# A gated mix of recurrent attention and a GEGLU feed-forward: buffers, order of a step, and the Wo group changed together

## The chip, the core and the metric

The kernel runs on one core of one Trainium2 chip. A core has five engines that run their own instruction streams and wait for each other through semaphores: TensorE (PE, matmuls into the eight PSUM banks), VectorE (DVE), ScalarE (ACT), GpSimd (POOL) and SyncE (SP, which here only issues DMAs). SP, ACT and POOL all issue DMAs, and each of them issues in the order of its own stream. The metric is the time of one execution on the device in microseconds.

## The reference: what is computed

Two branches work on the same x (2048 rows of 1024, bf16) and are mixed row by row:

```python
def _A_ref(x, mem0, Wq, Wk, Wv, Wo, seg_len):      # 32 heads of 128, seg_len 32, memory of 8 rows
    mem = mem0
    for s in range(n_seg):                          # 64 segments, one after the other
        h = concat([mem, x[s*32:(s+1)*32]])         # 40 rows
        q, k, v = h @ Wq, h @ Wk, h @ Wv            # each 1024 x (32 x 128)
        p = softmax(masked(q @ k.T * scale))        # rows see the memory and what is before them
        o = (p @ v) @ Wo
        mem = o[:8]                                 # the next segment's memory
        outs.append(o[8:])
def _B_ref(x, w_gate, w_up, w_down):                # 1024 -> 3584 -> 1024
    return gelu(x @ w_gate) * (x @ w_up) @ w_down
g = sigmoid((x * gate_w).sum(-1))
return g * a + (1 - g) * b
```

The attention branch is a recurrence: segment s+1 needs the first eight rows of segment s's output. Its weights (four matrices of 8 MB) don't fit in SBUF together.

## The kernel before, in words

**A planner, not hand-placed semaphores.** `op(eng, fn, rd, wr, lane)` records every operation with the byte ranges of SBUF, the PSUM banks and the DRAM pieces that it reads and writes. `_Prog.finish` (L118) derives the waits from that; `emit` (L135) writes each engine's stream in the order of recording. A DMA has a lane, that is, a semaphore. After its last operation SP waits for the last value of every lane (L153). What sets the order of the work is therefore the order of the calls, and what makes something wait is an overlap of bytes, banks or lanes.

**Four phases.** First the feed-forward branch, in four blocks of 512 rows (`for fb in range(NFB)`, L1060): 28 rounds j of gate and up matmuls into two pairs of banks, each followed by gelu on ACT and DVE into GT; then two passes `ps` over w_down in chunks of WD, the second pass backwards in the first three blocks so that the buffers left from the first are used at once. `mix` scales a finished bank by 1 - g and stores it to b_scr. Between rounds stand the preparations of x: `do_x` (PE transposes 128 rows; ACT and DVE copy them out in two forms; ACT issues the stores to xq_scr and xr_scr), `dot_x` (POOL multiplies by gate_w, DVE sums), `gate` (the sigmoid) and, in the last block, `begin(n)`, which loads the first attention weights into slots as FFN buffers come free.

Then step 0 of the recurrence with the projections of rows that need no memory ("fills", below), then 63 more steps, then the output phase: the remaining rows' Wo product (L1189), `blend` and the stores.

**Slots and pieces.** SBUF beyond the small tiles is 50 slots of 4096 bytes a partition. A piece is 512 KB of Wk, Wq, Wv or Wo: (m, u, i) is matrix m, half u of the heads, piece i of 8. Some pieces of the two halves share a slot (`PAIRS`, L317: two of k, two of q, five of v, five of o: 0, 1, 4, 5, 6). A shared slot is reloaded once a step, as soon as PE has done with it. `spent` (L440) counts the uses; neighbouring shared pieces are loaded by one DMA when the last of them is spent (`GROUPS`, L373, `load_group`, L422). SP issues all of these.

**A step.** `HEAD` and `BODY` (L324) give PE's order: k of the first half of the heads (r=0) pieces 0-3, q 0-1, the previous step's second Wo product pieces 4-7, q 2-3, v 0-3, k, q, v 4-7; then k, q (r=1), Wo (r=0), v (r=1), and the first four pieces of the second Wo product. In that second product the pieces come in the order 2, 3, 0, 1, 7, 4, 5, 6. `plan(s)` (L955) hangs everything else on this walk: `on(m, r, n, f)` runs f before piece n of (m, r). So `on("q", 0, 2, f)` puts f before q's third piece.

**Fills and stages.** Of each segment's 32 rows only the last 8 are not in the step's own projection; they are projected four segments at a time, in "fills" (L907). Each group of four steps needs six, listed in `FILL` (L945); steps 0 and 1 of four have two. The second of two is run and copied out by ACT at the start of the next step (`fill_evac`), into a stage of 1024 bytes a partition: stage 0 lies over hT0 and oRc, stage 1 over oRc and hT1. `fill_put` (L924) turns it on PE (L732), copies it back with DVE (L930) and stores it to qk_scr with a DMA on POOL (L932); it does nothing for v. Later in the same step, at ("q", 1, 1), ACT copies the step's own k, second half, into the same stage, and at ("o", 0, 0) PE turns that. `load_h` and `rest_o` use the bytes after that.

The last step moves five Wo pieces into slots of k and q (`late`), for the output phase.

Of the kernel before, what the change touches and what calls it, by code (L numbers as in the profile page):

```python
# [30 lines left out]
class _Prog:  # L31
# [73 lines left out]
    def finish(self):  # L105
        cnt = {e: 0 for e in self.ENGS}
        clocks = {e: {} for e in self.ENGS}
        for o in self.ops:
            if o.sem is None and o.need:
                cnt[o.eng] += 1  # L110
                o.sem, o.val, o.inc = self.sems[o.eng], cnt[o.eng], 1
        for o in self.ops:
            ck = clocks[o.eng]
            want = {}
            for d in o.deps:
                if ck.get(d.sem, 0) >= d.val:
                    continue
                if want.get(d.sem, (0, None))[0] < d.val:  # L118
                    want[d.sem] = (d.val, d)
            if want:  # L120
                items = sorted(want.items(), key=lambda kv: -kv[1][1].idx)
                ck = dict(ck)
                for s, (v, d) in items:
                    if ck.get(s, 0) >= v:
                        continue
                    o.waits.append((s, v))
                    for s2, v2 in d.clock.items():
                        if ck.get(s2, 0) < v2:
                            ck[s2] = v2
                    if ck.get(s, 0) < v:  # L130
                        ck[s] = v
                clocks[o.eng] = ck
            o.clock = ck

    def emit(self, block):  # L135
        self.finish()
        by = {e: [o for o in self.ops if o.eng == e] for e in self.ENGS}
        finals = [(ln[0], ln[1]) for ln in self.lanes.values()]
# [72 lines left out]
def bass_gated_mix__memory_aug_recurrent_mem_tr__geglu_ffn__prompt_kernel(  # L211
# [34 lines left out]
    with ExitStack() as es:  # L246
# [126 lines left out]
        GROUPS = {("k", 0): 2, ("q", 0): 2, ("v", 0): 3, ("v", 3): 2, ("o", 0): 1, ("o", 1): 1, ("o", 4): 3}  # L373
# [105 lines left out]
        WD = 4  # L479
# [6 lines left out]
        wd = [al(f"wd{i}", [128, WD, D]) for i in range(3)]  # L486
# [20 lines left out]
        xT = al("xT", [128, TB, 4, KC, SEG])  # L507
        assert cur[0] == edge(29)
# [3 lines left out]
        assert cur[0] == edge(43)  # L512
        osbF = [al(f"osbF{t}", [128, D], at=edge(28) + 2 * D * t) for t in range(2)]
        wdF = al("wdF", [128, NJ, D], at=edge(29))
        GT = al("GT", [128, NJ, FB])
        assert cur[0] == edge(50) and len(hosts) == 50
        for n in range(4):
            stage[f"X{n}"] = al(f"X{n}", [128, 512], at=edge(49) + 1024 * n)
        for n in range(3):
            stage[f"Y{n}"] = al(f"Y{n}", [128, 512], at=kT.off + 1024 * n)  # L520
        tp = [al(f"tp{t}", [128, FB], FP32, at=qkr.off + 4 * FB * t) for t in range(2)]
# [23 lines left out]
        def do_x(T):  # L545
            t = px[T % NPX]
            b = T % 2 + (4, 4, 0, 4)[T // TB]
# [4 lines left out]
            def f(e):  # L552
# [10 lines left out]
            op("dve", lambda e: e.tensor_copy(to, PBV[b].rearrange("p (k i c) -> p k i c", k=KC, i=4)[:, :, :, NR:SEG]),  # L563
               rd=[BK(b)], wr=[to_r])

            def put():
                op("act", lambda e: e.dma_start(xq_scr[T, :, :, :], xo[0].rearrange("p i k c -> p i (k c)")),
                   rd=[xo[1](0, 4)], wr=[("D", "xq", T)], lane=f"xw{x2}")
                if T > 0:
                    op("act", lambda e: e.dma_start(xr_scr[T], to.rearrange("p k i c -> p (k i c)")),  # L570
# [6 lines left out]
        def dot_x(T):  # L577
            t = px[T % NPX]
            op("pool", lambda e: e.tensor_tensor(out=gp[:, :], in0=t[:, :], in1=gwb[:, :], op=ALU.mult),
               rd=[t.r(), gwb.r()], wr=[gp.r()])  # L580
            op("dve", lambda e: e.tensor_reduce(dl[:, T:T + 1], gp[:, :], AX.X, ALU.add), rd=[gp.r()], wr=[dl.r(T, T + 1)])
# [35 lines left out]
        def load_wd(c):  # L617
            op("sp", lambda e: e.dma_start(wd[c % 3][:, :, :],
                                           B_w_down[c * WD * 128:(c + 1) * WD * 128, :].rearrange("(j p) f -> p j f", p=128)),
               wr=[wd[c % 3].r()], lane=f"wd{c % 3}")  # L620
# [11 lines left out]
        def gate(fb):  # L632
            c = slice(TB * fb, TB * fb + TB)
            r = lambda t: t.r(TB * fb, TB * fb + TB)
            op("act", lambda e: e.activation(gal[:, c], dl[:, c], ACTF.Tanh, scale=0.5), rd=[r(dl)], wr=[r(gal)])
            op("dve", lambda e: e.tensor_scalar(out=oml[:, c], in0=gal[:, c], scalar1=-0.5, scalar2=0.5, op0=ALU.mult, op1=ALU.add),
# [11 lines left out]
        jF = {1: (0, 1), 6: (1, 3), 13: (3, NWD)}  # L648

        def load_wdF(c):  # L650
            op("sp", lambda e: e.dma_start(wdF[:, c * WD:(c + 1) * WD, :],
                                           B_w_down[c * WD * 128:(c + 1) * WD * 128, :].rearrange("(j p) f -> p j f", p=128)),
               wr=[wdF.r(c * WD * D, (c + 1) * WD * D)], lane=f"wd{c % 3}")
# [9 lines left out]
        op("pe", tr_mem, rd=[pm.r(), mT.r(), ident.r()], wr=[BK(6)])  # L663
        op("dve", lambda e: e.tensor_copy(mS[:, 72:80], PBV[6][:, 64:64 + NB]), rd=[BK(6)], wr=[mS.r(72, 80)])
        op("dve", lambda e: e.tensor_copy(memT[:, :], PBV[6][:, 0:64]), rd=[BK(6)], wr=[memT.r()])

# [40 lines left out]
        def blend(T):  # L707
# [4 lines left out]
            op("act", lambda e: e.dma_start(of[128 * T:128 * T + 128, :], t[:, 0:D]), rd=[t.r(0, D)], wr=[("D", "out", T)], lane=f"ol{T % 4}")  # L712
# [242 lines left out]
        def plan(s):  # L955
# [11 lines left out]
            if s == 0:  # L967
                on("v", 0, 0, lambda: fill0("v", 0, B2, "X3"))
# [15 lines left out]
            if s == 0:  # L984
                on("k", 1, 0, lambda: load_v(0, slice(0, 1)))
            on("k", 1, 1 if s == 0 else 4, lambda: evac(bank_of["v", 0], vA, "act"))
            if s == 0:
                on(*('k', 1, 4), lambda: scores(ua, False))
                on("k", 1, 1, lambda: fill0("k", 1, A1, "X0"))
                on(*('q', 1, 2), lambda: attend(ua))  # L990
                on("k", 1, 4, lambda: fill_put("k", 1, 0, "X0"))
                on("q", 1, 0, lambda: fill0("q", 1, B1, "X1"))
                on("q", 1, 2, lambda: fill_put("q", 1, 0, "X1"))
                on("q", 1, 4, lambda: load_qk(0, 1))
                on("q", 1, 4, lambda: fill0("v", 1, B2, "X2"))
                on("q", 1, 4, lambda: load_r(1) if NG > 1 else None)
                on("o", 0, 4, lambda: load_v(0, slice(1, 2)))
# [34 lines left out]
            if last:  # L1032
                late = [lambda k=k, n=n: load_piece(moved[k], k, f"moved{n}") for n, k in enumerate(moved)]
                on("q", 0, 4, *late[:3])
                on("v", 0, 4, *late[3:])
# [16 lines left out]
            if two:  # L1052
                on("q", 0, 2, lambda: fill_put(*fl[1], ua, SS), **nx)
# [6 lines left out]
        for fb in range(NFB):  # L1060
            HB, DN = ((0, 1, 2, 3), (4, 5, 6, 7)) if fb % 2 == 0 else ((4, 5, 6, 7), (0, 1, 2, 3))
            for j in range(NJ):
# [24 lines left out]
                if todo and j % 3 == 2:  # L1087
                    mix(*todo.pop(0))
                if fb == 0 and j < TB:
                    puts.pop(0)()  # L1090
                    dot_x(j)
                    load_x(j + NPX)
                if fb == 0 and j == TB - 1:
                    load_w(3)
                    load_w(4)
                    for n in range(3):
                        load_wd(n)
                if fb == 0 and j == TB:
                    gate(0)
# [3 lines left out]
                if fb < NFB - 1 and j in (6, 11, 16, 21):  # L1103
                    do_x(T)
                    dot_x(T)
                    load_x(T + NPX)
                if fb < NFB - 1 and j == 25:
                    gate(fb + 1)
# [7 lines left out]
            if fb + 1 == NFB:  # L1116
                for n in (11, 12, *range(20, 28)):
                    begin(n)
            for ps in range(NPS):
# [4 lines left out]
                for c in range(NWD)[::-1 if back else 1]:  # L1124
                    w = wdF if end else wd[c % 3]
# [14 lines left out]
                    if not end:  # L1140
                        if back and c == 3:
                            load_xT(fb + 1)
                        nc_ = c - 3 if back else c + 3
                        if 0 <= nc_ < NWD:
                            load_wd(nc_)
                    elif ps == NPS - 1:
                        for f in {1: [lambda: fill0("k", 0, A0, "Y0")],
                                  2: [lambda: fill0("k", 0, A1, "Y1", 1, hR1), lambda: fill_put("k", 0, 0, "Y0")],
                                  3: [lambda: fill0("q", 0, XO, "Y2"), lambda: fill_put("k", 0, 1, "Y1")],
                                  4: [lambda: fill_put("q", 0, 0, "Y2")], 5: [lambda: load_qk(0, 0)]}.get(c, ()):  # L1150
                            f()
                        for n in (29 + 2 * c, 30 + 2 * c, 43 + c):
                            if n < 49:
                                begin(n)
# [3 lines left out]
        begin(28)  # L1158
# [22 lines left out]
        for b in range(NBK):  # L1181
            ob = orb[0]
            for hf in range(2):
# [10 lines left out]
                while mixed < NT and mixed < 2 * (2 * b + hf) + 4:  # L1194
# [6 lines left out]
                   rd=[ob.r(lo, hi)], wr=[("D", "out", T) for T in range(4 * b, 4 * b + 4)], lane=f"or{hf}")  # L1201
# [37 lines left out]
```

## Time and profile before

| | |
|---|---|
| median of three runs | 2202.14 us (2199.84 to 2203.8) |
| the profiled execution | 2196.2 us, its span 2194.4 us |
| feed-forward, 12 to 620 us | PE busy 595.9 of 608; DMA share 0.52 |
| end of it and step 0, 620 to 671 us | PE busy 36.6 of 51; granted clock 0.87 |
| steps 1 to 61, 671 to 2079 us | PE busy 1300.1 of 1408; DMA share 0.93, 347 GB/s |
| last two steps, 2079 to 2131 us | PE busy 40.4 of 52; granted clock 0.89 |
| output phase, 2131 to 2194.4 us | PE busy 55.6 of 63.4 |

The stretches were chosen by the first and last instruction of each phase. "PE busy" is the union of its matmuls; the DMA share is the mean busy share of the core's 16 DMA engines; the granted clock is the share of TensorE's full clock that the profile records. In the lines of waits, "A <- B: 24.5, 34, 1.6" says that A's engine sat idle for 24.5 us in all, 34 times, at most 1.6, until B was done. In the timeline a line has start, duration, engine, line of the code, what is written and read, how many instructions, and in brackets the idle time before and who ended it. A DMA's "us to landing" is the time from its issue to its semaphore.

### The profile page before, as it was taken

Reading aid. Unit: us, or ns where it says so; the run is one execution under the profiler, and the core shown is the slowest. Engines: PE = TensorE matmul, PEld = TensorE weight load, DVE = VectorE, ACT = ScalarE, POOL = GpSimd, SP = SyncE. Lnnn points to the kernel's source line nnn. Section 1 sums busy time; section 2 is a strip of 40 time slices with the busy share of each in tenths; the row PEclk is TensorE's granted clock in tenths of the full one; section 3 lists DMA queues with packets and bytes.
Section 4 is the critical chain, followed back from the end, with each engine's and each line's share of the span. In section 5 each row is a group of like instructions: output and inputs, shape, how many; then the busy total and the mean of one; then the engine's idle time right before and its main releaser. Section 6 shows DMA issues by size and latency. Waiting matters only on the chain.

```text
span 2194.4 us, 69744 instructions
## 1 busy us (share of the span) xinstructions
PE 2033.8 (93%) x31337; PEld 972.6 (44%) x31365; DVE 1027.1 (47%) x2657; ACT 551.6 (25%) x1142; POOL 443.1 (20%) x835
## 2 busy tenths in 40 slices
PE   8999999999979899998999999999899999999878
PEld 4444444444434444444444444444444444444345
DVE  5615616436224445444454454544544545445444
ACT  3303303213112222222222222222223222222210
POOL 3000100000022222322223223222232322222110
PEclk9999999999999999999999999999999999999999
DMA  9352264364587999999899999999999999999997
GB/s 308 128 192 89 91 219 124 84 234 165 185 307 285 336 338 344 346 358 345 328 357 348 356 354 342 356 343 360 344 340 349 346 338 358 337 348 347 337 334 269
DMA packets 180106, 640.23 MB, mean 292 GB/s; under 512 B 25144, under 2 KB 74936, under 8 KB 138976
## 3 DMA queue, kind: packets, MB, share of 16 engines
q1 hardware_dynamic: 150800, 595.52, 74.3%
q0 software_dynamic: 17472, 26.41, 3.9%
q10 hardware_dynamic: 11536, 13.85, 1.8%
q8 instruction: 246, 4.03, 0.7%
q14 instruction: 52, 0.43, 0.1%
HBM read 600.00 MB, written 50.27 MB: 296 GB/s over the span
## 4 chain that ended last, share of the span: by engine, by line
PE 65%; DMA 22%; DVE 6%; ACT 3%; issue 2%; POOL 1%; ACTq 0%; SPq 0%; POOLq 0%
PE pb L834 24%; PE pb L1068 14%; DMA wall<-o_scr 9%; PE pb L1134 7%; PE pb L850 5%; PE pb L732 3%; PE pb L867 3%; PE pb L907 3%; PE pb L1189 3%; DMA o_scr<-oRc 2%; DMA sl<-v_scr 2%; DMA wd<-in_B_w_down_dram 2%; DMA qk_scr<-1S 2%; DVE oT L718 1%; DMA v_scr<-kS 1%
## 5 line engine op out<-in xcount | busy, mean ns | idle before, releaser
L834 PE MATMUL pb<-sl,hT 128*32 128x512 bf16 x12288 | 761.8, 382 | 21.4 <-DVE hT L894 8.8
L834 PEld LDWEIGHTS pb<-sl,hT 128*32 128x32 bf16 x12288 | 309.4, 97 | 328.1 <-DVE hT L894 27.6
L907 PE MATMUL pb<-sl,hR 128*32 128x512 bf16 x3072 | 213.5, 384 | 7.1 <-DMA sl<-in_A_Wk_dram 3.8
L1068 PE MATMUL pb<-xT,wg 128*128 128x512 bf16 x896 | 213.4, 381 | 5.4 <-DVE GT L1084 4.1
L1068 PE MATMUL pb<-xT,wu 128*128 128x512 bf16 x896 | 212.5, 380 | 0.0
L817 POOL COPY oRc<-oT 128x128 bf16<-128x128 bf16 x128 | 96.6, 755 | 407.6 <-DVE oT L718 407.6
L867 PE MATMUL pb<-wall,oT 128*32 128x256 bf16 x4056 | 151.0, 278 | 28.4 <-DMA wall<-o_scr 24.5
L1134 PE MATMUL pb<-wd,GT 128*128 128x512 bf16 x657 | 147.2, 382 | 7.1 <-DMA wd<-in_B_w_down_dram 6.3
L718 DVE COPY part<-pb 64x256 f32<-64x256 f32 x96 | 40.4, 421 | 237.3 <-PE pb L867 237.3
L850 PE MATMUL pb<-wall,oT 128*32 128x512 bf16 x2048 | 145.8, 381 | 5.8 <-issue 0.2
L1076 ACT ACTIVATE s<-pb 128x512 f32<-128x512 f32 x112 | 66.8, 596 | 308.8 <-PE pb L1068 269.9
L1077 DVE SCALAR_TENSOR_TENSOR tp<-s,pb 128x512 f32<-128x512 f32 x112 | 76.8, 686 | 131.9 <-ACT s L1076 131.9
L867 PEld LDWEIGHTS pb<-wall,oT 128*32 128x32 bf16 x4056 | 97.4, 97 | 87.8 <-ACT oT L715 26.3
L1068 PEld LDWEIGHTS pb<-xT,wg 128*128 128x128 bf16 x896 | 86.8, 98 | 110.8 <-DVE GT L1084 8.0
L1068 PEld LDWEIGHTS pb<-xT,wu 128*128 128x128 bf16 x896 | 87.9, 98 | 106.6 <-issue 1.6
L768 ACT ACTIVATE E<-pb 128x320 bf16<-128x320 f32 x128 | 56.0, 437 | 311.0 <-DVE pb L767 311.0
L718 DVE COPY kT<-pb 128x512 bf16<-128x512 bf16 x128 | 54.4, 425 | 159.9 <-PE pb L732 159.8
L936 POOL COPY kT<-qkr 128x128 bf16<-128x128 bf16 x128 | 37.2, 291 | 423.1 <-DVE tAB L780 222.9
L715 ACT ACTIVATE oS<-pb 128x512 bf16<-128x512 f32 x63 | 37.6, 597 | 336.0 <-PE pb L834 336.0
L780 DVE STREAM_TRANSPOSE tAB<-pAB 128x128 bf16<-128x128 bf16 x512 | 114.0, 280 | 4.4
L1081 DVE SCALAR_TENSOR_TENSOR tp<-tp,pb 128x512 f32<-128x512 f32 x112 | 77.0, 687 | 78.7 <-ACT tp L1080 78.7
L718 DVE CAST oT<-pb 128x160 bf16<-128x160 f32 x256 | 76.4, 320 | 75.6 <-PE pb L800 75.5
(113 smaller groups left out, 2208.5 us busy)
## 6 DMA issues: line engine op xcount, KB each, us to landing
sl<-v_scr SPq DMA_DIRECT2D x64, 1536.0 KB, 10.0
wall<-o_scr SPq DMA_DIRECT2D x63, 1536.0 KB, 9.2
wall<-o_scr SPq DMA_DIRECT2D x131, 512.0 KB, 5.1
sl<-k_scr SPq DMA_DIRECT2D x64, 1024.0 KB, 5.8
sl<-q_scr SPq DMA_DIRECT2D x64, 1024.0 KB, 8.3
sl<-v_scr SPq DMA_DIRECT2D x64, 1024.0 KB, 9.6
wd<-in_B_w_down_dram SPq DMA_DIRECT2D x27, 1024.0 KB, 6.7
wdF<-in_B_w_down_dram SPq DMA_DIRECT2D x7, 1024.0 KB, 8.9
```

The lines of the kernel that those rows point to most:

```text
L718: op("dve", lambda e: e.tensor_copy(o, i), rd=rd, wr=wr, after=after)
L780: return [op("dve", lambda e, c=c: e.transpose(tAB[:, c + 32 * k:c + 32 * k + 4 * w].rearrange("p (j x) -> p j x", j=4)[:, :, 0:32], pAB[: ...
L817: op("pool", lambda e: e.tensor_copy(oRc[:, :, 16 * u:16 * u + 16].rearrange("p c x -> p x c"), oT[:, :, :, 32:40].rearrange("p g j c -> p ...
L834: ins = e.matmul(PB[bk][32 * g:32 * g + 32, :], lhsT=h[:, i, :], rhs=w[:, g * 512:(g + 1) * 512], start=(n == 0), stop=(n == 7))
L850: ins = e.matmul(PB[XO][32 * g:32 * g + 32, :], lhsT=oT[:, j, x, 0:32], rhs=wall[:, na:nb + 1:nb - na, c:c + 256], start=(n == 0 and hp == 0),
L867: ins = e.matmul(PB[XO][32 * g:32 * g + 32, 256 * b:256 * b + 256], lhsT=oT[:, j, x, 0:32], rhs=w[:, c:c + 256], start=False, stop=(n % 4 ...
L907: ins = e.matmul(PB[b][32 * g:32 * g + 32, :], lhsT=h[:, k[2], :], rhs=w[:, g * 512:(g + 1) * 512], start=(n == 0), stop=(n == 7))
L1068: ins = e.matmul(PB[bk][:, 0:FB], lhsT=w[:, kc, cc:cc + 128], rhs=xT[:, :, :, kc, :].rearrange("p t i c -> p (t i) c"), start=(kc == 0), s ...
L1076: op("act", lambda e, hg=hg: e.activation(s1[:, :], hg, ACTF.Square, scale=SQ), rd=[BK(bg)], wr=[s1.r()])
L1077: op("dve", lambda e, hg=hg, t=t: e.scalar_tensor_tensor(out=t[:, :], in0=s1[:, :], scalar=1.0, in1=hg, op0=ALU.add, op1=ALU.mult), rd=[BK ...
L1081: op("dve", lambda e, hu=hu, t=t: e.scalar_tensor_tensor(out=t[:, :], in0=t[:, :], scalar=1.0, in1=hu, op0=ALU.add, op1=ALU.mult), rd=[BK( ...
L1134: ins = e.matmul(PB[bank[2 * k + hf]][:, :], lhsT=GT[:, j, tb * 128:(tb + 1) * 128], rhs=w[:, x, hf * 512:(hf + 1) * 512], start=(j == end ...
```

## The change

What it does, part by part:

- **The later turn.** `fill_put` of the second fill goes from before q's third piece (r=0) to before its sixth, past two pieces of q, four of v, four of k and one of q on PE, and past a_scr's store on POOL.
- **Wo pieces 4, 5, 6** are loaded as a group of two (4, 5) and one (6), each when its pieces are spent.
- **w_down** comes in 14 half chunks through six buffers of half the size instead of seven chunks through three; in the backward pass xT's load is recorded after the last of them.
- **Gate, x and the memory in the feed-forward.** `dot_x` is split: the product on POOL goes ahead of the puts or of do_x, the sum on DVE goes to the next round. `gate` is split, its DVE part and the four small stores a round or two later. The copy of the rows for xr and the store to xr_scr (now on POOL) belong to `put`. The first block's four transposes use four banks instead of two. The memory's transposes go from before the first round to round 4.
- **Layout and start of the recurrence.** xT moves from slots 27-28 to 41-42, the last block's w_down to slots 27-40; so slot 42 (a Wo piece) instead of 28 (a Wk piece) is the one loaded late, in step 0. The first v fill moves from step 0 into the last w_down pass, with its own stage Y3 and its vB load; in step 0 the fills of k, q, their puts and the loads of qkr and vB stand earlier.
- **The end.** The five late Wo pieces are all issued behind v's last load. SP's final waits leave out what other waits imply. The output stores are tracked by half rows, so that two stores of the last rows don't wait for one another.

```diff
+        self.last = clocks["sp"]
...
-        finals = [(ln[0], ln[1]) for ln in self.lanes.values()]
+        finals, ck = [], dict(self.last)
+        for ln in sorted(self.lanes.values(), key=lambda ln: -ln[2].idx):
+            if ck.get(ln[0], 0) < ln[1]:
+                finals.append((ln[0], ln[1]))
+                for m, v in [*ln[2].clock.items(), (ln[0], ln[1])]:
+                    ck[m] = max(ck.get(m, 0), v)
...
-        GROUPS = {..., ("o", 0): 1, ("o", 1): 1, ("o", 4): 3}
+        GROUPS = {..., ("o", 0): 1, ("o", 1): 1, ("o", 4): 2, ("o", 6): 1}
...
-        WD = 4
+        WD = 2
+        NWB = 6
...
-        wd = [al(f"wd{i}", [128, WD, D]) for i in range(3)]
+        wd = [al(f"wd{i}", [128, WD, D]) for i in range(NWB)]
...
-        xT = al("xT", [128, TB, 4, KC, SEG])
-        assert cur[0] == edge(29)
         for c in (0, 1, 2):
...
+        assert cur[0] == edge(41)
+        xT = al("xT", [128, TB, 4, KC, SEG])
+        osbF = [al(f"osbF{t}", [128, D], at=edge(42) + 2 * D * t) for t in range(2)]
+        wdF = al("wdF", [128, NJ, D], at=edge(27))
...
+        stage["Y3"] = al("Y3", [128, 512], at=vB.off)
...
-            b = T % 2 + (4, 4, 0, 4)[T // TB]
+            b = T + 4 if T < TB else T % 2 + (4, 4, 0, 4)[T // TB]
...
-            op("dve", lambda e: e.tensor_copy(to, PBV[b]...[:, :, :, NR:SEG]), rd=[BK(b)], wr=[to_r])
             def put():
+                op("dve", lambda e: e.tensor_copy(to, PBV[b]...[:, :, :, NR:SEG]), rd=[BK(b)], wr=[to_r])
                 op("act", lambda e: e.dma_start(xq_scr[T, :, :, :], ...), lane=f"xw{x2}")
                 if T > 0:
-                    op("act", lambda e: e.dma_start(xr_scr[T], ...), lane=f"xv{x2}")
+                    op("pool", lambda e: e.dma_start(xr_scr[T], ...), lane=f"xv{x2}")
...
-            op("act", lambda e: e.dma_start(of[...], t[:, 0:D]), rd=[...], wr=[("D", "out", T)], lane=f"ol{T % 4}")
+            op("act", lambda e: e.dma_start(of[...], t[:, 0:D]), rd=[...], wr=[("D", "out", T, 0), ("D", "out", T, 1)], lane=f"ol{T % 4}")
...
             if s == 0:
-                on("v", 0, 0, lambda: fill0("v", 0, B2, "X3"))
...
-                on("k", 1, 0, lambda: load_v(0, slice(0, 1)))
+                on("k", 1, 0, lambda: fill0("k", 1, B0, "X0"))
...
-                on("k", 1, 1, lambda: fill0("k", 1, A1, "X0"))
+                on("k", 1, 4, lambda: fill0("q", 1, A1, "X1"))
...
-                on("q", 1, 0, lambda: fill0("q", 1, B1, "X1"))
-                on("q", 1, 2, lambda: fill_put("q", 1, 0, "X1"))
-                on("q", 1, 4, lambda: load_qk(0, 1))
+                on("q", 1, 0, lambda: fill_put("q", 1, 0, "X1"))
+                on("q", 1, 0, lambda: load_qk(0, 1))
...
-                on("o", 0, 4, lambda: load_v(0, slice(1, 2)))
+                on("o", 0, 0, lambda: load_v(0, slice(1, 2)))
+                on("q", 0, 4, lambda: begin(42))
...
-                on("q", 0, 4, *late[:3])
-                on("v", 0, 4, *late[3:])
+                on("v", 0, 5, *late)
...
             if two:
-                on("q", 0, 2, lambda: fill_put(*fl[1], ua, SS), **nx)
+                on("q", 0, 5, lambda: fill_put(*fl[1], ua, SS), **nx)
...
+                if fb == 0 and 0 < j <= TB:
+                    dot_r(j - 1)
                 if fb == 0 and j < TB:
+                    dot_m(j)
                     puts.pop(0)()
-                    dot_x(j)
...
                 if fb < NFB - 1 and j in (6, 11, 16, 21):
+                    dot_m(T)
                     do_x(T)
-                    dot_x(T)
                     load_x(T + NPX)
+                if fb < NFB - 1 and j in (7, 12, 17, 22):
+                    dot_r(T)
                 if fb < NFB - 1 and j == 25:
-                    gate(fb + 1)
+                    gate_a(fb + 1)
+                if fb < NFB - 1 and j == 27:
+                    gate_b(fb + 1)
...
-                        if back and c == 3:
-                            load_xT(fb + 1)
-                        nc_ = c - 3 if back else c + 3
+                        nc_ = c - NWB if back else c + NWB
                         if 0 <= nc_ < NWD:
                             load_wd(nc_)
+                        if back and c == NWB:
+                            load_xT(fb + 1)
...
-                        for f in {1: [fill0 k 0], 2: [fill0 k 0 (G 1), put], 3: [fill0 q 0, put],
-                                  4: [put], 5: [load_qk(0, 0)]}.get(c, ()):
+                        for f in {3: [fill0 k 0], 5: [fill0 k 0 (G 1), put], 7: [fill0 q 0, put],
+                                  9: [put, lambda: fill0("v", 0, A0, "Y3")],
+                                  10: [load_qk(0, 0)], 13: [lambda: load_v(0, slice(0, 1))]}.get(c, ()):
                             f()
-                        for n in (29 + 2 * c, 30 + 2 * c, 43 + c):
+                        begin(27 + c)
+                        if c % 2 and c < NWD - 1:
+                            begin(43 + c // 2)
...
-                   rd=[ob.r(lo, hi)], wr=[("D", "out", T) for T in range(4 * b, 4 * b + 4)], lane=f"or{hf}")
+                   rd=[ob.r(lo, hi)], wr=[("D", "out", T, hf) for T in range(4 * b, 4 * b + 4)], lane=f"or{hf}")
```

## The prediction

> **What bounds the kernel now.** I read the page first: the span, the busy shares, the DMA line and the chain.
>
> ```profile
> span 2194.4 us, 69744 instructions
> PE 2033.8 (93%) x31337; PEld 972.6 (44%) x31365; DVE 1027.1 (47%) x2657; ACT 551.6 (25%) x1142; POOL 443.1 (20%) x835
> ...
> DMA  9352264364587999999899999999999999999997
> ...
> PE 65%; DMA 22%; DVE 6%; ACT 3%; issue 2%; POOL 1%; ACTq 0%; SPq 0%; POOLq 0%
> ```
>
> TensorE (PE) is busy 93% of the time, and from slice 13 on the DMA engines are nearly full as well. In the 64 steps (671 to 2079 us by stretches: 1408 us, PE busy 1300, DMA share 0.93, 347 GB/s) neither has much room: a step takes 21 to 25 us, and what PE waits for is small and sits in a few places. So the second view is the waits of PE:
>
> ```profile
> PE pb L891 <- DVE a_bf L882: 31.7, 33, 1.0
> PE pb L867 <- DMA wall<-o_scr: 24.5, 34, 1.6
> PE pb L732 <- ACT 1S L715: 6.8, 13, 1.9
> PE pb L1134 <- DMA wd<-in_B_w_down_dram: 6.3, 6, 2.2
> PE pb L1068 <- DVE GT L1084: 4.1, 3, 1.9
> PE pb L732 <- ACT 0S L715: 4.2, 11, 0.6
> ```
>
> Total, times, longest. The change leaves the first alone and reaches for the other five: 46 us in all, and no more can be won directly. The third view is the timeline of one step with two fills, because a step's order is moved there:
>
> ```profile
> 1046.84 0.40 PE L732 MATMUL pb<-ident,0S 128*128 128x128 bf16 x4 [0.62 <-ACT 0S L715]
> 1047.99 0.76 POOL L932 DMA_DIRECT2D qk_scr<-0S  x1 [0.81 <-DVE 0S L930]
> 1050.70 0.40 PE L732 MATMUL pb<-ident,oS 128*128 128x128 bf16 x4
> 1054.73 0.60 ACT L715 ACTIVATE 0S<-pb 128x512 bf16<-128x512 f32 x1
> 1057.06 0.40 PE L732 MATMUL pb<-ident,0S 128*128 128x128 bf16 x4
> ```
>
> The stage 0S is used twice in a step: the second fill is turned out of it (1046.84) and sent to qk_scr (1047.99); then ACT puts k's second half into the same bytes (1054.73) and PE turns that (1057.06). ACT may write only when the DMA has landed, at 1054.32 here. The chain shows a step where it landed too late:
>
> ```profile
> 977.36 9.12 DMA qk_scr<-1S
> ...
> 986.56 0.61 ACT 1S L715
> ...
> 987.21 0.40 PE pb L732 x4
> ```
>
> PE sat idle 1.87 us before that turn. This store is nearly on the path already. The DMA view says how long such transfers take:
>
> ```profile
> wall<-o_scr SPq DMA_DIRECT2D x63, 1536.0 KB, 9.2
> ...
> a_scr<-a_bf POOLq DMA_DIRECT2D x64, 64.0 KB, 8.9
> ...
> qk_scr<-0S POOLq DMA_DIRECT2D x15, 128.0 KB, 7.0
> qk_scr<-1S POOLq DMA_DIRECT2D x15, 128.0 KB, 7.3
> ...
> hR<-xr_scr POOLq DMA_DIRECT2D x15, 64.0 KB, 8.9
> ```
>
> **The change part by part** (sums against the profiled execution: span 2194.4, 2196.2 us with what lies around it; the median of the runs, 2202.1, is 5.9 above that, and I carry the 5.9 over).
>
> *The later turn.* It goes from before q's third piece to before its sixth. Gain: PE no longer waits for ACT at the first turn; by place in the step that is 8.1 of the 11.0 us in the two rows of 0S and 1S (the other 3.0, with the 1.87, are at the second turn). Cost: between the two places PE has 3.16 us of work (1046.84 to 1050.70, less three pieces of 12 matmuls, 0.7), of which 0.33 is the turn itself: the turn comes 2.83 us later, and the store with it. DVE's copy (0.42) and the bank SS have room there (DVE idles 2.3 us before 1051.1, the mask that takes SS comes 1.3 us on), and on POOL only a_scr's issue changes places with it. The wait that grows is ACT's for the store. The two turns of one stage start 10.0 us apart in nearly all of the 30 steps that have a second fill (10.7 at most, the second's own idle time left out). From this go 0.65 (ACT's copy and its hand-over), 2.83, and 1.15 from turn to issue (1046.84 to 1047.99): 5.37 us are left for the store. Its 30 landings took 6.3 to 9.1, 7.2 in the mean. So all 30 would be late. Behind ACT's copy stand q's copy and two of oT, behind the turn stands all of PE, and behind PE the wall loads on SP; so it is paid in full. The landing time in the new place is not in the trace. Lower end 6.3, the quickest of the 30: 25 us of stalls over the 30 steps. Upper end 8.9, the DMAs that POOL issues at about the new time (a_scr, hR): 103 us. I take 7.6, nearer the store's own rows because a qkr load that POOL issues just behind the first v load, in the steps of the fourth kind, still lands in 6.3 (median): 64 us. With 8.1 saved and 3.0 that is there already: **+53** (+14 to +92).
>
> [...]
>
> *Wo pieces 4, 5 and 6 as two and one.* Of the 24.5 us for wall, 13 (20 steps) are at pieces 4 to 6 by place in the step, the rest at piece 1, which is loaded as before. All three pieces come over the same full queue, so piece 6 lands no earlier; but PE can do 4 and 5 before it: min(wait, 0.49) a step, 8 us. One more DMA a step on SP: its 0.32 us of issue lies beside the queue's backlog. At worst all 63 cost it, 20 us; I take 2. The stalls above delay PE more than the loads, so some of the remaining wall waits go: −5. **−11** (−16 to +12).
>
> *w_down in six buffers of half the size.* A load now has five half chunks (5 × 1.73) instead of two chunks (2 × 3.45) of matmuls as its lead: 8.6 against 6.9 us, and half the bytes; loads took 6.7, up to 9.0 with xT's load ahead, which now goes behind the last one. The 6.3 us go, and with them 1.7 us of half clock (granted 0.83 over 160 to 170 us). I take **−7** (−8 to +1; 27 more issues on SP cover nobody's wait).
>
> *Gate sums, puts, transposes.* The three waits for GT (4.1 us) follow ACT's issue of the xr store (2.56 us at 40.5, 1.49 at 214.5) beside DVE's 1.21 us reduction. The store goes to POOL, which is idle there (7% busy from 12 to 620 us), and the reduction to the next j: **−3.5** (−4.1 to +1.1, as four 0.28 us copies enter DVE's first four rounds, which take 3.83 us against PE's 3.45). The first block's 0.8 us wait for xT is set to nothing: the memory's transposes and these copies come back in the loop.
>
> *Step 0.* Slot 28 is no longer loaded last: the 3.8 us wait for Wk, 0.3 behind it, 1.0 for osbF and the 1.7 for vB have their cause removed. What is late next is POOL's chain: stores of k and q one after the other (3.8 and 2.4 us), qkr (5.4), then v's stores, and behind them now load_v and put_rest, which PE waits for (5.1 us today). That wait moves up by only 1 or 2 us, and PE, early, waits longer for it. **−4** (−12 to +4).
>
> *The end.* The last two output stores no longer wait for one another (2188.08 and 2190.42: 1.8 us), and SP's final waits shrink from 1.2 us. PE's 5.9 us wait for v at 2124.7 goes as the five late pieces come behind it, but DVE runs without a gap from 2173.5, so at most 0.7 of it reaches the end. **−3.5** (−6 to 0).
>
> Sum: 53 − 11 − 7 − 3.5 − 4 − 3.5 = **+24**, 2202.1 + 24 = **2226 us**.
>
> **Rivals.**
> *The store lands in time (faster).* With a landing mean of 6.3 the term is 25 − 11 = +14, and with the other five (−29) the sum is −15: 2187. It decides at 6.8, where the stalls (40 us) equal all gains. For it: transfers get lighter when PE pauses, and a_scr is now ahead, not behind. Against: 24 of the 30 took longer than 6.4 today with less in front. [...]
>
> *The store takes as long as its new neighbours.* 8.9 us: 103 − 11 − 29 = +63, 2265. For it: hR, issued 5.5 us after k's load, lands only 14.2 us after it. On top the clock may drop: an idle 2.18 us (at 162.5) was followed by half clock for 3.4 us, while 1.87, 1.92 and 1.94 were not. [...]
>
> *The split does nothing.* The three pieces land together at the end of the backlog: 8 us less gain, 2234, inside the range.
>
> **How the numbers follow.** 0.2% (4.4 us) is about what a measurement of this kernel can tell. Landing between 7.0 and 8.5 (forecast, 2206 to 2256): 0.60. Longer: 0.14. Between 6.7 and 7.0, where all cancels: 0.08. Shorter, the first rival: 0.18. So slower 0.74, same 0.08, faster 0.18. The range runs from the first rival's 2187 to the second's 2265 with a little clock loss: 2187 to 2268, leaving out the empty-queue case and a general loss of clock.
>
> **What would show it.** Later turn: the rows L732 <- ACT 0S and 1S grow from 11 to about 60 us, now before the second turn of the stage, ACT's wait there is for DMA qk_scr<-0S and 1S, and periods grow in two steps of four. Split: wall waits under 15 us. w_down: the row wd is gone. GT: under 1 us. Step 0: no wait for Wk. End: the last two stores issue within 0.6 us of each other. The prediction is wrong if the store lands in under 6.8 us, or if the loads behind a late PE catch up, so that the wall waits vanish and pay for the stalls.

## The result, and the profile after

The changed kernel takes 2261.3 us (median; 2260.6 to 2269.9) where the kernel before took 2201.0 beside it: a ratio of 1.030 (95% interval 1.027 to 1.032), 60 us slower. The forecast was 24 us slower. The profiled execution is 2260.6 us with a span of 2258.8, 64.4 more than the span before.

The page of the changed kernel: span, busy shares, the DMA engines in 40 slices, and the chain by engine.

```profile
span 2258.8 us, 69792 instructions
...
PE 2060.8 (91%) x31337; PEld 984.2 (44%) x31365; DVE 1027.2 (45%) x2657; ACT 548.6 (24%) x1142; POOL 451.3 (20%) x850
...
DMA  9362463374588989989889898998989889898998
...
PE 60%; DMA 25%; DVE 6%; ACT 4%; issue 2%; SPq 2%; POOL 0%; ACTq 0%; DVEq 0%; POOLq 0%
```

TensorE is busy for 27 us more with the same matmuls, so some of them ran slower; the other 37 us are idle time. The waits of PE say where (total, times, longest; line numbers are 6 to 17 higher than before, L741 was L732):

```profile
PE pb L741 <- ACT 1S L724: 37.5, 15, 3.5
...
PE pb L741 <- ACT 0S L724: 31.6, 15, 3.4
PE pb L1151 <- DMA wd<-in_B_w_down_dram: 13.1, 3, 5.3
...
PE pb L876 <- DMA wall<-o_scr: 8.8, 20, 1.1
PE pb L916 <- DMA sl<-v_scr: 5.5, 1, 5.5
...
PE pb L1074 <- DVE GT L1090: 3.5, 8, 0.9
```

The two rows of the stages were 11.0 us and are 69.1, now 2.3 us in each of the 30 steps with a second fill. The wait for wall fell from 24.5 to 8.8. The wait for w_down (wd), which was to go, doubled. One step of the timeline:

```profile
898.21 0.80 POOL L941 DMA_DIRECT2D qk_scr<-1S  x1 [1.68 <-DVE 1S L939]
...
906.76 0.60 ACT L724 ACTIVATE 1S<-pb 128x512 bf16<-128x512 f32 x1 [4.54 <-DMA qk_scr<-1S]
...
907.41 0.40 PE L741 MATMUL pb<-ident,1S 128*128 128x128 bf16 x4 [3.00 <-ACT 1S L724]
```

The store leaves at 898.21 and takes 8.47; ACT waits 4.54 for it, and PE 3.00 for ACT. The DMA view (KB each, median us to landing):

```profile
wall<-o_scr SPq DMA_DIRECT2D x194, 512.0 KB, 5.7
...
wall<-o_scr SPq DMA_DIRECT2D x63, 1024.0 KB, 8.1
wd<-in_B_w_down_dram SPq DMA_DIRECT2D x54, 512.0 KB, 5.6
...
a_scr<-a_bf POOLq DMA_DIRECT2D x64, 64.0 KB, 8.5
...
qk_scr<-0S POOLq DMA_DIRECT2D x15, 128.0 KB, 7.6
qk_scr<-1S POOLq DMA_DIRECT2D x15, 128.0 KB, 7.8
```

By phase, with the same boundaries as before: the last w_down matmul ends at 633.4 us instead of 620.9, so the feed-forward lost 12.4 (of which 1.9 is the v fill that moved into it); the first 61 steps of the recurrence after step 0 took 1471.2 instead of 1408.4 (+62.8); step 0 and the end gained 8 and 2.5. In the steps the waits make +58.1 for the stages and −15.7 for wall. PE's own busy time there grew from 1300.1 to 1325.1 us with the same matmuls; these 25 us are clock. Other short waits make −5. The stretch of the steps in three runs: after, the kernel before with the later turn alone (e2), and after with PE kept busy in the stall (e5; columns: us, busy times of five engines, granted clock, DMA share, GB/s; the kernel before had 1.00, 0.93 and 347).

```profile
675.00:2146.20 1471.20, 1325.11 (x26810) 638.42 (x26806) 689.67 (x2102) 378.81 (x850) 373.62 (x741) 0.97 0.89 332
```

```profile
666.70:2158.60 1491.90, 1332.54 (x26814) 637.34 (x26810) 688.98 (x2102) 378.47 (x850) 373.82 (x741) 0.97 0.89 327
```

```profile
671.10:2136.40 1465.30, 1346.24 (x27114) 655.74 (x27110) 689.92 (x2102) 378.53 (x850) 374.92 (x741) 1.00 0.89 333
```

Added up from the trace's clock records, the clock stood at half for 8 us of the steps before and for 76 us after, in pieces of 3.4 us or twice that. The e5 run kept PE busy with added matmuls, so its busy time there holds 45.9 us of them.

### The profile page after: what moved, and what is told of

It is laid out like the page before. It is cut to its first block, busy times and chain, and to the rows that moved or that the text cites. A ratio compares the mean times of both kernels' runs of the same rounds, so it can differ in the third digit from the quotient of the medians.

```text
span 2258.8 us, 69792 instructions
## 1 busy us (share of the span) xinstructions
PE 2060.8 (91%) x31337; PEld 984.2 (44%) x31365; DVE 1027.2 (45%) x2657; ACT 548.6 (24%) x1142; POOL 451.3 (20%) x850
## 3 DMA queue, kind: packets, MB, share of 16 engines
q0 software_dynamic: 17952, 27.40, 4.0%
q10 hardware_dynamic: 9376, 12.87, 1.6%
## 4 chain that ended last, share of the span: by engine, by line
PE 60%; DMA 25%; DVE 6%; ACT 4%; issue 2%; SPq 2%; POOL 0%; ACTq 0%; DVEq 0%; POOLq 0%
PE pb L843 19%; PE pb L1074 13%; PE pb L1151 8%; DMA wall<-o_scr 7%; DMA qk_scr<-1S 5%; PE pb L859 5%; DMA qk_scr<-0S 5%; PE pb L876 4%; PE pb L916 4%; DMA sl<-v_scr 3%; PE pb L741 3%; DMA wd<-in_B_w_down_dram 2%; ACT vA L724 1%; PE pb L900 1%; DVE a_bf L891 1%
## 5 line engine op out<-in xcount | busy, mean ns | idle before, releaser
L859 PE MATMUL pb<-wall,oT 128*32 128x512 bf16 x2048 | 168.1, 432 | 3.4
L1151 PE MATMUL pb<-wd,GT 128*128 128x512 bf16 x657 | 151.8, 392 | 13.9 <-DMA wd<-in_B_w_down_dram 13.1
L876 PE MATMUL pb<-wall,oT 128*32 128x256 bf16 x4056 | 146.5, 276 | 12.1 <-DMA wall<-o_scr 8.8
L1151 PEld LDWEIGHTS pb<-wd,GT 128*128 128x128 bf16 x672 | 67.3, 101 | 98.5 <-DMA wd<-in_B_w_down_dram 14.6
```

The lines of the kernel that those rows point to most:

```text
L859: ins = e.matmul(PB[XO][32 * g:32 * g + 32, :], lhsT=oT[:, j, x, 0:32], rhs=wall[:, na:nb + 1:nb - na, c:c + 256], start=(n == 0 and hp == 0),
L876: ins = e.matmul(PB[XO][32 * g:32 * g + 32, 256 * b:256 * b + 256], lhsT=oT[:, j, x, 0:32], rhs=w[:, c:c + 256], start=False, stop=(n % 4 ...
L1151: ins = e.matmul(PB[bank[2 * k + hf]][:, :], lhsT=GT[:, j, tb * 128:(tb + 1) * 128], rhs=w[:, x, hf * 512:(hf + 1) * 512], start=(j == end ...
```

## The experiments

Ratios are to the kernel before, run beside each variant on the same chip; a difference between two ratios is given in us of 2202. A profiled execution can lie some us off its median (e12's by 10.0), so effects are taken from the ratios and places from the traces.

**Each cause taken back (e1 to e4).**

e1:
```diff
-                on("q", 0, 5, lambda: fill_put(*fl[1], ua, SS), **nx)
+                on("q", 0, 2, lambda: fill_put(*fl[1], ua, SS), **nx)
```


> The kernel after, with only the second fill's turn back before q's third piece. Theory (the late store costs the 69 us of waits for ACT's copy into 0S and 1S, and the half clock behind these waits, about 22 us, and the late PE spares it some wall waits): the two rows of L741 fall back to about 11 us (-58), L850's busy time from 168 to about 146 us (-22), the wall waits come back in part (+8). 2261 - 72 = 2189 us. Rival (the clock in the steps is lost for another reason, such as the split, and the wall waits come back in full, +16): 2261 - 58 + 16 = 2219 us or more.

Measured: 2203.2 us, ratio 0.999 (0.997 to 1.001); 58 us (medians) to 68 us (ratios) under the full change. The waits of e1:

```profile
PE pb L876 <- DMA wall<-o_scr: 20.6, 33, 1.7
PE pb L1151 <- DMA wd<-in_B_w_down_dram: 13.7, 3, 4.9
PE pb L741 <- ACT 1S L724: 9.6, 15, 1.7
PE pb L741 <- ACT 0S L724: 9.0, 13, 1.5
```

The stalls and most of the half clock went (19 us of it left in the steps), and PE's busy time in the steps fell from 1325.1 to 1304.2 us, by 21 where the theory had 22. But the stage waits went to 18.6 us and not to 11, and wall came back by 12 rather than 8, so the time fell between the theory's 2189 and the rival's 2219. What the rival says of the clock is not so.

e2, the kernel before with the same line moved the other way, from ("q", 0, 2) to ("q", 0, 5):

> The kernel before, with only the later turn. Theory: +58 us of waits for ACT's copies, +22 us of half clock behind them, about -9 us of wall waits, which a late PE no longer has: 2201 + 71 = 2272 us, so above the full change. Rival (the term as forecast, +53, no clock, with 5 of wall waits going): 2249 us. Rival 2 (the later turn costs much less without the other parts): 2240 us or less.

Measured: 2264.1 us, ratio 1.025 (1.022 to 1.028), 56 to 60 us slower. The waits of the stages:

```profile
PE pb L732 <- ACT 1S L715: 37.7, 15, 3.8
PE pb L732 <- ACT 0S L715: 35.7, 15, 3.7
```

They make 73.4 us, wall 18.1, and half clock 92 us in the steps. The time lies between theory and first rival. The later turn alone costs as much as the whole change; what the other parts gain and lose comes to about nothing (e1).

e3:
```diff
-                if fb < NFB - 1 and j == 27:
+                if fb < NFB - 1 and j == 25:
                     gate_b(fb + 1)
```


> The kernel after, with the gate's DVE part and its four small stores back in round 25 instead of 27. Theory (the small stores stand right ahead of the w_down loads and hold them back): the three waits for wd, 13.1 us, go, and the half clock behind them, about 8 us: 2261 - 21 = 2240 us. Rival (loads of half the size from six buffers are late by themselves): the waits stay, 2261 us.

Measured: 2247.8 us, ratio 1.020 (1.018 to 1.022). No wait for wd at all; the feed-forward ends at 612.6 instead of 633.4. The feed-forward gains 20.8 us, the theory's 21, and by the ratios the whole gains 22; by the medians it is 13. The steps are not shorter in this profile, which has 10 us more half clock there than after. So the doubled wd wait came with the later gate, not with half-size loads.

e4, both taken back:

> The kernel after, with both taken back: the turn before q's third piece and the gate's stores in round 25. Theory (the two losses are separate and add up): 2189 - 21 = 2168 us, under both kernels. Rival (one of the two is no loss, or the other parts of the change gain nothing): 2189 to 2200 us.

Measured: 2183.4 us, ratio 0.992 (0.989 to 0.994): under both kernels, but 15 above the sum, because e1, from which the sum starts, had itself come out 14 above its 2189. Between e3 and e4 the turn is 62 to 64 us, between e1 and e4 the gate 16 to 20.

**What the half clock costs (e5).**

```diff
+        def spin():
+            def f(e):
+                for _ in range(10):
+                    ins = e.matmul(PB[XO][:, 0:320]..., lhsT=ident[:, :], rhs=mS[:, :]..., start=True, stop=True)
...
+                if s % 4 in (1, 2) and s < 60:
+                    on("o", 0, 0, spin)
```


> The kernel after, with ten added matmuls of 320 columns (nothing reads their result) in front of the stage's second turn, in the two steps of four that have a second fill: TensorE does useless work for about 1.4 us of the 2.3 us stall. Theory (the half clock comes from the stalls): the remaining gaps are about 0.9 us, the half clock within the steps falls from 76 us towards the 8 us of the kernel before, and 15 to 20 us of time go although nothing was taken from the path: 2261 - 18 = 2243 us. Rival (the half clock has another cause, the power of the matmuls for instance): half clock as before or more, 2261 us or slower.

Measured: 2256.0 us, ratio 1.024 (1.022 to 1.027). The waits:

```profile
PE pb L885 <- DMA wall<-o_scr: 18.8, 31, 1.5
PE pb L741 <- ACT 1S L724: 17.0, 14, 2.0
PE pb L741 <- ACT 0S L724: 10.1, 14, 1.4
```

Half clock in the steps fell from 76 to 14 us, and the first Wo product, which stands right behind the stall, from 168.1 to 146.5 us (145.8 before the change). Without the added matmuls PE is busy for 1346.2 − 45.9 = 1300.3 us in the steps, as before the change. So the stalls cause the half clock, and it costs PE 25 us: that part of the theory holds. But the steps became only 6 us shorter. Wall waits took back 10 us (8.8 after the change, 18.8 here), as a PE at full clock (granted 1.00 instead of 0.97) comes earlier to pieces that are no earlier. The added matmuls (45.9 us, with 27.1 of stall left: 73.0 against 69.1) took 4 more, and other short waits 5. Of the 25 us, then, the end sees 6, or about 10 without the added matmuls' own 4.

**Who issues the store (e6b).**

```diff
-            op("pool", lambda e: e.dma_start(qk_scr[:, 4 * G:4 * G + 4, m4, :], ...), lane="fq")
+            op(eng, lambda e: e.dma_start(qk_scr[:, 4 * G:4 * G + 4, m4, :], ...), lane="fqa" if eng == "act" else "fq")
...
-                on("q", 0, 5, lambda: fill_put(*fl[1], ua, SS), **nx)
+                on("q", 0, 5, lambda: fill_put(*fl[1], ua, SS, "act"), **nx)
```


> The kernel after, with the second fill's store issued by ScalarE's queue instead of GpSimd's. Theory A (the store is slow because all 16 DMA engines are nearly full, whoever issues it): it still takes 6 to 8 us, the waits for ACT's copies stay near 69 us, 2255 to 2270 us. Theory B (it is slow because of GpSimd's way of issuing): it takes 3 to 5 us, less than the 5.4 us that it has, the waits fall to a few us and the half clock with them, 2261 - 80 = 2181 us.

Measured: 2373.3 us, ratio 1.078 (1.075 to 1.080). Neither theory: the store takes longer from ACT (10.5 and 11.0 us in the median, 7.6 and 7.8 from POOL), and the waits for ACT's copies grow from 69.1 to 147.5 us. The page's rows of the queues (packets, MB, share of 16 engines), and the store's rows in the DMA view:

```profile
q0 software_dynamic: 16512, 23.46, 3.5%
q10 hardware_dynamic: 25216, 16.80, 2.3%
```

```profile
qk_scr<-0S ACTq DMA_DIRECT2D x15, 128.0 KB, 10.5
qk_scr<-1S ACTq DMA_DIRECT2D x15, 128.0 KB, 11.0
```

After, q0 (POOL's) had 17952 packets and 27.40 MB, q10 (ACT's) 9376 and 12.87. So the 30 stores are 1440 packets on POOL's queue and 15840 on ACT's: 48 against 528 for 128 KB, some 2.7 KB against 0.25. The 48 took 7.7 us in the mean, the 528 took 10.7. Whether the number of packets makes the difference is not shown: queue and packet size change together here, and no run tries the same queue with another packet size.

**What in the later gate holds the loads (e7, e9, e12).** e7 is the kernel before with its whole `gate` in round 27 instead of 25.

> The kernel before, with only the gate (tanh, DVE part and four small stores) of the next block moved from round 25 to 27. Theory (the small stores right ahead of the w_down loads hold them back): the waits for wd grow from 6 to 15 to 20 us with half clock behind them, 2202 + 15 = 2217 us. Rival (they hurt only with loads of half the size): 2202 us.

Measured: 2237.0 us, ratio 1.016 (1.014 to 1.018), 33 to 35 slower, twice the theory's price:

```profile
PE pb L1134 <- DMA wd<-in_B_w_down_dram: 34.1, 8, 11.4
```

With three buffers of 1 MB this move costs more than the later gate does with six of half a MB (16 to 23 us), though e7 also moves the tanh. The stretches around 274 us in the profile after show what happens; the four stores are issued from 270.75 to 272.34 and land at 281.5 to 282.0, the loads at 270.33, 272.05 and then every 1.73:

```profile
270.00:274.00 4.00, 4.00 (x20) 1.78 (x19) 0.46 (x3) 0.00 (x0) 3.23 (x5) 1.00 0.47 140
274.00:282.00 8.00, 6.60 (x30) 2.84 (x29) 0.00 (x0) 0.00 (x0) 1.03 (x1) 1.00 1.17 43
282.00:286.00 4.00, 0.01 (x1) 0.02 (x2) 0.00 (x0) 0.00 (x0) 0.00 (x0) 0.83 0.49 167
286.00:292.00 6.00, 6.00 (x16) 2.22 (x17) 0.00 (x0) 0.00 (x0) 0.00 (x0) 0.55 1.04 383
```

The load ahead of the stores lands in 3.81 us, the one issued at 272.05 only at 285.94, 4 us after the last store. While the stores are under way, the DMA engines count as fully busy (1.17) and move 43 GB/s; once they have landed, 383. By what mechanism so little data holds the loads back, no run shows. PE stands still from 280.7 to 286.0 and goes on at half clock until 291.4 (granted 0.55 from 286 to 292). Each of the four stores writes 128 elements of 4 bytes.

e9 was to move the stores alone, to round 4 of the next block, with the turn back at q's third piece:
```diff
+        def gate_st(fb):
...
             for T in range(TB * fb, TB * fb + TB):
                 op("pool", lambda e, T=T: e.dma_start(gt_scr[...], gal[:, T:T + 1]), ...)
...
+                if fb > 0 and j == 4:
+                    gate_st(fb)
```


> The kernel after, with the turn back before q's third piece; the gate's DVE part stays in round 27, and its four small stores alone go to round 4 of the next block, where no w_down load follows them. Theory (the stores, not the arithmetic, hold the loads back): no waits for wd, as with the whole gate in round 25: 2183 us, within 5. Rival (DVE's part or the order on GpSimd is to blame): the three waits of 4 to 5 us stay, 2203 us.

Measured: 2203.6 us, ratio 1.000 (0.998 to 1.002), wd waits 11.8 us, which looks like the rival. It is not: in the trace the stores still leave at 268.70 us. GpSimd had nothing ahead of them in its stream, so a later place in the code was no later time. The run is a second e1. e12 moves what the stores wait for:
```diff
+        def gate_c(fb):
             op("dve", lambda e: e.tensor_scalar(out=gal[:, c], in0=gal[:, c], ...))
             for T in range(TB * fb, TB * fb + TB):
                 op("pool", lambda e, T=T: e.dma_start(gt_scr[...], gal[:, T:T + 1]), ...)
...
+                if fb > 0 and j == 4:
+                    gate_c(fb)
```


> The kernel after, with the turn back before q's third piece. Of the gate, 1 - g is still made in round 27; the DVE operation that makes g, which the four small stores wait for, goes to round 4 of the next block, and with it the stores (in the run e9 the stores stood in round 4 in the code, but GpSimd had nothing ahead of them and issued them at 268.70 us, as before). Theory (the stores hold the w_down loads back): no waits for wd, 2183 us, as with the whole gate in round 25. Rival (what DVE does in round 27 is to blame): three waits of 4 to 5 us, 2203 us.

Measured: 2181.5 us, ratio 0.990 (0.987 to 0.993). There is no wait for wd, and the loads go at 4 to 5 us each; the same stretch:

```profile
263.00:271.00 8.00, 7.95 (x37) 3.62 (x37) 0.00 (x0) 0.00 (x0) 0.00 (x0) 1.00 0.91 298
```

DVE's 1 − g is still in round 27, so it is not that part of DVE's work. The one operation that makes g moved together with the stores; that it is the stores and not this operation rests on the loads above, which land only behind them. The feed-forward ends at 610.1 us, 10.8 before the kernel before. Even with the gate in round 25 (e4) the stores (issued from 254.86, landing at 265.4 to 266.0) stretch the first loads to 8 us, without a wait of PE.

**The split (e8)**, the kernel before with only ("o", 4) loaded as 2 and ("o", 6) as 1:

> The kernel before, with only the three Wo pieces loaded as two and one. As forecast (without the stalls' share): wall waits 24.5 - 8 + 2 = 18.5 us, 2202 - 6 = 2196 us. Rival 1 (the three pieces land together): no change, 2202 us. Rival 2 (one more DMA a step on a full queue delays what stands behind it, the loads and the stores of the next step): some us slower, up to 2210 us.

Measured: 2194.9 us, ratio 0.996 (0.995 to 0.998), 8 to 9 us faster; wall waits fall from 24.5 to

```profile
PE pb L867 <- DMA wall<-o_scr: 16.7, 27, 1.6
```

which is 7.8, the 8 us of the forecast's min(wait, 0.49). Rivals 1 and 2 fall by the medians and the ratio; the 2 us for the added issue did not show. The profiled execution of e8 can't confirm the gain: its steps (1409.0 us) are as long as those before (1408.3), as other short waits took the place of those for wall.

**How the loss grows with the way (e10, e11).** As e9, with the turn at ("q", 0, 3) and at ("k", 0, 4).

> As e9, with the turn one piece (0.25 us) later, before q's fourth. By the same sum as for the whole shift: the wait before the first turn shrinks by up to 0.25 us in 26 steps (-5), the five stores that already land late and a few that become late add about 1.5: 3 us under e9, 2180 us. Rival (any shift only costs): 2186 us or more.

> As e9, with the turn six pieces (1.5 us) later, before k's fifth; about half of the way of the change. The store then has 8.2 - 1.5 = 6.7 us. With the landings of the run with both parts back (5.2 to 8.5, 20 of 30 over 6.7) the stalls are 16 us, with landings 0.35 longer 24 us, against 15 us at both turns there; none over 2 us, so no half clock from them: 1 to 9 us above e9, 2189 us. Rival (a cost in proportion to the way, half of 58 to 64 us): 30 us above e9, 2213 us.

Measured: 2198.2 (0.9985, 0.9969 to 1.0001) and 2207.6 us (1.003, 1.001 to 1.005) beside e9's 2203.6. e11 is 4 us over e9 by the medians and 6 by the ratios, as summed, and not 30: half of the way costs a tenth or less of the whole. (Both forecasts started from 2183 for e9, which became 2203.6, so they are read as distances from e9.) Its stage waits are

```profile
PE pb L744 <- ACT 1S L727: 13.4, 13, 1.9
...
PE pb L744 <- ACT 0S L727: 11.2, 11, 1.4
```

24.6 us where the sum gave 16 to 24, with none over 2. The price follows the store's landing against the time left for it, 6.7 us here by the forecast's sum and 5.37 in the full change, where the stage waits are 69.1 us. That no half clock would come of it held only in part: the steps have 29 us of it (14 in e9, 20 in e12), and three of the nine pieces stand right behind stage waits of 1.2 to 1.7 us. e10's gain of 4 to 5 us has the expected sign; but its interval overlaps e9's, and so does that of e11.

**Both ideas together (e13, e14).** e13 is e4 with the turn at ("q", 0, 3), e14 is e12 with it.

> The kernel after, with the gate's DVE part back in round 25 and the turn before q's fourth piece, one later than before the change. The two gains add: 2183 - 5 = 2178 us, 23 us under the kernel before. Rival (the gain of 5 us was chance): 2183 us.

> As e12, with the turn before q's fourth piece, one later. If the stores are the cause: 2178 us as well, 2176 if the loads behind the gate in round 25 still lost something. If not: 2198 us, as with one piece later and the gate as in the change.

Measured: 2177.8 us, ratio 0.989 (0.986 to 0.992), and 2176.3 us, ratio 0.988 (0.986 to 0.991). Both are faster than both kernels, by 24 and 25 us against the kernel before. That the turn's one piece adds to e4 and e12 is within their intervals; that the gate's stores and the place of the turn are what has to be undone is not.

## Why the prediction was right or wrong

- **The later turn (+53): the mechanism was right, a term was missing.** The time left was taken as 5.37 us and the landing as 7.6; the 30 stores took 6.7 to 8.9, 7.7 in the mean, 2.3 over, and the stalls came to 69.1 us in all where the working had 64 (30 × 2.23 is 67). By the runs the term is 56 to 68 us. What the working left out of its sum, and so put at nothing, is the half clock behind these stalls. The text had seen it once (2.18 us at 162.5) and put it into the second rival only, as a thing that may come on top; 23 of the 30 stalls were over 2 us, half clock in the steps grew from 8 to 76 us, and PE's busy time by 25. e5 shows the half clock to come from the stalls, and 6 to 10 us of the 25 to reach the end. The empty queue that the range leaves out was not met in the steps: in the trace before, the store issued at 647.75 landed in 2.4 us beside a DMA share of 0.22, and after the change, with the share at 0.89 in the steps, none of the 30 landed in under 6.7. The second rival, a landing of 8.9, did not happen; that its time (2265) is near the result is chance.
- **The split (−11): right in size.** −8 alone, for its own −8 + 2 of the sum. The −5 that stalls were to take off the wall waits is 6.4 in e2, which has the later turn without the split. In the changed kernel wall falls by 15.7 in all; without the half clock (e5) it falls by 5.7 only.
- **w_down in half chunks (−7): wrong in sign, through another line of the change.** The failing step is "The 6.3 us go". They were put down to lead and size, with xT's load in front. For the 4.1 us of them that stood behind xT's load (the waits of 2.18 and 1.94 us) this held: they are gone. The loads' times of 6.7 to 9.0 were read, but not what stood in front of the first load, which PE awaited for 1.47 us at 124.05: the gate's four small stores, issued from 108.96 and landed at 117.4 to 121.1. That load was issued at 117.17, and from there to 121.1 the DMA engines moved 20 GB/s, in the 8 us behind it 347. The change puts these stores two rounds later, right among the loads, and PE then waited three times, 13.1 us in all, each time for a load issued behind the first of them. The prediction gave the move of `gate`'s DVE part and of its DMAs no cost of its own. By the ratios it cost 16 to 23 us. With the stores out of the way (e12) the feed-forward ends 10.8 us earlier than before, against the forecast 7 + 3.5.
- **Gate sums, puts (−3.5): the row GT fell from 4.1 to 3.5 only**, as eight short waits of up to 0.9 in place of three; its gain can't be told apart from the w_down term in e12's 10.8.
- **Step 0 (−4): right**, −6 when the v fill's 1.9 us are counted where they went. Wk's wait is gone, and v's stands there instead, 5.5 us, as named.
- **The end (−3.5): −2.5.** The last two stores leave at 2255.39 and 2255.97, 0.58 apart.

In the traces two steps of the working fail, each by some 21 us. The feed-forward came to +10.5 (without the v fill) where −7 and −3.5 were set down. The 61 steps came to +62.8 where 53 − 11 = 42 was set down: 5 more of stalls, 25 of clock, 5 less for wall and 5 less of other waits; had the clock stayed up, 6 to 10 of the 25 would have gone by e5, where the wall waits come back by 10. So the loss is 60 us and not 24, although the one large term was nearly right in its stalls; that the sum had the right direction is owed to that term.

## What to carry to other kernels

When a change moves a step, list every DMA that moves with it and look at what each one lands among, not only at the engine time: here, with four stores of 512 bytes under way, a load of 512 KB took 13.89 us where the one ahead of them took 3.81. When a buffer is used twice, compare the store's landing with the time left for it and not with the distance moved: in these runs a shift of 1.5 us (e11) cost 4 to 6 us and the whole of 2.83 us 56 to 68, with 69.1 us of stage waits and 25 us of clock in it. And check a moved operation's start in the trace before reading the run: in e9 the stores stood in a later round of the code and still left at 268.70 us, as GpSimd had nothing ahead of them; with what they wait for moved as well (e12), the wait for wd was gone.

## What the runs showed of the hardware

- Four stores of 128 elements of 4 bytes took 9.7 to 10.7 us each (at 271 us after the change), and while they were under way the DMA engines moved 43 GB/s instead of 383, with their busy share at 1.17. In e12, where no w_down load follows them, they still take 8 to 12 us and PE waits for none.
- Stalls of 2.0 to 2.5 us were followed within 7 us by half clock in 10 of 17 cases after the change, and in two more it set in during the stall's last 0.7 us. In the steps the half clock came in pieces of 3.4 us or twice that. 2 us is no sharp limit: e11 and e12 have 29 and 20 us of half clock in the steps with no stage wait over 2.0 us.
- The 128 KB store took 7.7 us in the mean from GpSimd's queue and 10.7 from ScalarE's, with eleven times as many packets.
- Of the 25 us that the half clock cost PE in the steps after the change, the end saw 6 to 10: in e5, with 14 us of half clock instead of 76, the steps were 6 us shorter, and the waits for wall were 18.8 us instead of 8.8.
